# Attention feeding a gated feed-forward layer: 36 attention chunks in place of 40, load chains of their own, tile 2's gated sums kept on chip, and other figures in the ordering model

## The chip, the cores and the metric

The kernel runs on one core of a Trainium2 chip. The metric is the device time of one execution in microseconds (us), lower is better. Times are medians of several runs; the profile is that of one further execution.

## The reference

The attention of 8 batches, 8 heads, 576 queries of 64 elements looks at keys and values that are averaged over groups of 8, so 72 keys for each head. Its output, 4608 rows of 512, is the input of a feed-forward layer with two input matrices.

```python
k_p = k.reshape(B, H, Sp, 8, D).mean(axis=3)          # B, H, D = 8, 8, 64; S = 576; Sp = 72
v_p = v.reshape(B, H, Sp, 8, D).mean(axis=3)
scores = np.matmul(q, k_p.transpose(0, 1, 3, 2)) / np.sqrt(D)
attn = np.exp(scores - np.max(scores, axis=-1, keepdims=True))
attn = attn / (np.sum(attn, axis=-1, keepdims=True) + 1e-09)
x = np.matmul(attn, v_p).transpose(0, 2, 1, 3).reshape(4608, 512)
out = ((x @ w_a) * (x @ w_b)) @ w_out                 # 512 x 1536, 512 x 1536, 1536 x 512
```

## The kernel before

**Arithmetic.** Every matrix product is made of three matmuls in fp32r: each operand is split into a high part and a remainder (`hh` and `hl`, `xh` and `xl`, `qh` and `ql`), and high·high, high·low and low·high are summed in PSUM. ACT casts the high part (line 247, `copy`), and DVE or POOL subtracts it (line 225, `low_part` through `tt`).

**Feed-forward tiles.** The 4608 rows are nine tiles of 512 (t = 0 to 8); the 1536 inner columns are twelve chunks f of 128. "in t f" is 24 matmuls of 512 columns into the banks `psa` and `psb` (line 276, `pe`); `gate` multiplies the two banks into a gated sum; "out t f" is 12 matmuls into four `acc` banks. Tiles 0 and 1 are the opening, in which the weights arrive and are converted from 64-bit words (`convert_weights`), split (`split_weight`) and stored to DRAM as `jd` and `od`. Tile 2 is an ordinary tile that reads split weights back (`jab`, `jo_later` and `wo`). Tiles (3, 4), (5, 6) and (7, 8) are pairs, in which seven block products replace eight ("both p f", banks `bank_psa`, `bank_psb`, `bank_att`; `fold` adds them up on DVE, `fold_second` on POOL as `temp_p` and `temp_h`). The weights that these products need (`sums`, made by `sums_of_weights` of `wab`) are made once in tiles 1 and 2 and stored to `jd`; the sums of x (`sums_of_x`) are made ahead of each pair. The second tile of a pair, seven of tile 1's twelve gated sums and all of tile 2's are written to DRAM (`later<-gated`, `later<-temp_h`) and fetched again (`fetch_gated`, `back<-later`, then `hh` and `hl`).

**Attention.** `load_keys` and `load_values` pool a batch's k and v (`kraw`, `vraw`, two buffers `kv0` and `kv1`) and write the block-diagonal `kdiag` and `vdiag` (two of each, by batch parity). `chunk(i)` takes 128 or 64 queries: the load of `qraw`, split to `qh` and `ql`, two groups of 6 score matmuls (`psc`), maximum, exponential, sum and scaling on `s`, split to `pr` and `rem`, 10 transposes (`ptr`), and, once a block of up to 256 rows is whole, the value matmuls (`po`). A batch has 576 rows, so it is cut into four chunks of 128 and one of 64. Results go to `xh` and `xl` (tiles 0 and 1) or by `xo` to DRAM (`xd`).

**What sets the order.** The class `Schedule` (lines 71 to 180) issues all instructions of all engines from chains (Python generators) by a list scheduler: each operation has a modelled cost (line 53 on: `FIXED`, `EACH`, `BYTE`, `LAND`), and of those that can start within `SLACK` the one with the lowest rank goes first. Ranks come from `due`, the modelled time at which a step of the main chain falls. The engines then run their instructions in just that order; a wait of one holds all behind it. Operations that DVE and POOL both can do go to whichever the model says starts first. SP issues all DMAs through one queue. `tmps` is a pool of six 128x512 buffers, shared by `qraw`, `gated`, `back`, `xo`, `y` and others.

Of the kernel before, what the change touches and what calls it, by code (L numbers as in the profile page):

```python
# [17 lines left out]
POOL = 8  # L18
# [13 lines left out]
def chunks_of(b):  # L32
    sizes = [128, 128, 128, 128, 64] if b % 2 == 0 else [64, 128, 128, 128, 128]
    out, o = [], 0
    for n in sizes:
        out.append((o, n))
        o += n
    return out


# [5 lines left out]
NTMP = 6  # L46
LAG = 5

# [14 lines left out]
BYTE, LAND, AHEAD = 1 / 330e3, 1.4, 1.5  # L63


class Op:


    def __init__(self, engines, run, writes, reads, cost, rank=None, pair=False):
        self.engines, self.run, self.writes, self.reads = engines, run, writes, reads  # L70
        self.cost, self.rank, self.pair = cost, rank, pair
        self.end = None


class Schedule:
# [15 lines left out]
    def ready(self, op):  # L91
# [9 lines left out]
        return max(op.at, op.asked)  # L101
# [29 lines left out]
    def issue(self, engine, start, op):  # L131
# [5 lines left out]
        else:  # L137
# [10 lines left out]
            self.free[engine] = end  # L148
# [12 lines left out]

    def run(self):
# [26 lines left out]
def attn_moe_kernel(ctx: ExitStack, tc: tile.TileContext, q, k, v, vr, wa, wb, wo, out):  # L189
# [64 lines left out]
    def dma(out, in_, rank=None):  # L254
# [46 lines left out]
    def raw(name, f):  # L301
        if name == "o":
            return wo_first[:, f * 512:(f + 1) * 512] if f < 8 else wo_rest[:, (f - 8) * 512:(f - 7) * 512]
        at = (f % 4) * 1024 + (512 if name == "b" else 0)
        return wab[f // 4][:, at:at + 512]
# [6 lines left out]
    area = {name: work[:, x * 1024:(x + 1) * 1024] for x, name in enumerate(("a", "b", "o"))}  # L312

    flat = [(b, o, n) for b in range(B) for o, n in chunks_of(b)]
    tile_of = [(b * S + o) // NT for b, o, n in flat]
    early = sum(t == 0 for t in tile_of)
    blocks, start = [], 0

    def cut(chunks, limit):
        best = None  # L320
        for x in range(1, len(chunks) + 1):
            total = sum(flat[c][2] for c in chunks[:x])
            if total > limit:
                break
            cost, rest = cut(chunks[x:], limit) if x < len(chunks) else (0, [])
            cost += max(total, 2 * P)
            if best is None or cost < best[0]:
                best = cost, [chunks[:x]] + rest
        return best

    while start < len(flat):
        stop = start
        while stop < len(flat) and flat[stop][0] == flat[start][0] and tile_of[stop] == tile_of[start]:
            stop += 1
        blocks += cut(list(range(start, stop)), BLOCK)[1]
        start = stop
    block_of = [x for x, block in enumerate(blocks) for _ in block]
# [9 lines left out]
    streamed = {("o", t * NF + f) for t in [*range(2, STD), *(t1 for _, t1 in PAIRS)] for f in range(NF)}  # L347
# [35 lines left out]
    for t in range(2, STD):  # L383
        order += [("in", t, f) for f in range(NF)] + [("out", t, f) for f in range(NF)]
# [15 lines left out]
    stored |= {t * NF + f for t in [*range(2, STD), *(t1 for _, t1 in PAIRS)] for f in range(NF)}  # L400
    uses, upcoming = [], {name: [] for name in "aboh"}
    for kind, t, f in order:
# [16 lines left out]
    def chunk_due(i):  # L419
        b, o, n = flat[i]  # L420
# [5 lines left out]
        share = (b * S + o + n - group[0] * NT) / (NT * len(group))  # L426
# [4 lines left out]
    def queries(i):  # L431
        b, o, n = flat[i]
        return q[b, :, NK * o:NK * (o + n)].rearrange("p (g s) -> p g s", g=NK)

    def load_early():
        yield dma(early_q[:, 0, :, :flat[0][2]], queries(0))
# [4 lines left out]
        yield dma(early_q[:, 1, :, :flat[1][2]], queries(1))  # L441
# [5 lines left out]
        for i in range(2, early):  # L447
            yield dma(early_q[:, i, :, :flat[i][2]], queries(i))
            mark("early_q", i)

    def convert_weights(name):
        words = area[name].rearrange("p (c w) -> p c w", w=2)
        hi, lo = words[:, :, 1], words[:, :, 0]
        yield W(("early_q", early - 1))
        for f in range(NF):
            lead = due["in", 0, f] - (4.0 if name == "o" else 14.0) + (0.5 if name == "b" else 0.0)
            yield dma(area[name], w_dram[name][:, f, :].bitcast(I32), lead - 4.0)
# [6 lines left out]
            tag = yield from take(tmps)  # L464
            low = tmp(tag, f"wlow_{name}{f}", I32)
            one = act(w, hi.bitcast(F32), lambda: nc.scalar.activation(w, hi.bitcast(F32), AF.Abs, scale=SHRINK), lead)
            yield one
            yield act(low, lo, lambda: nc.scalar.activation(low, lo.bitcast(U32), AF.Copy, scale=2.0**-29), lead)
# [13 lines left out]
    holder, turn_of = {}, {"a": 0, "b": 0}  # L482
    spare, held = {}, {"o": 0, "h": 0}

    def buffer_of(name, x):
# [5 lines left out]
        return jab[n][:, "ab".index(name)]  # L491
# [19 lines left out]
    def split_weight(name, x):  # L511
# [10 lines left out]
        hi, lo = to[:, 0], to[:, 1]  # L522
# [735 lines left out]
```

## Time and profile before

| | |
|---|---|
| median of 3 runs | 1108.34 us (1105.13 to 1108.48) |
| the profiled execution | 1113.18 us |
| its span from first to last instruction | 1111.4 us |
| mean granted TensorE clock | 0.968 |
| TensorE matmuls (records) | 4936 |
| DMA | 262.55 MB, mean 236 GB/s |

The span falls into six stages, told by the first matmul of a kind on PE: the opening until `psa_0_0` (52.8 us), until tile 1 joins with `psa_1_5` (142.7 us), tiles 0 and 1 until `psa_2_0` (343.0 us), tile 2 until the first `bank_` (491.6 us), pair 0's products until the first `acc` of tile 4 (696.2 us), and the rest. Each row of a table by windows gives the stretch, its length, the busy time and number of instructions of PE, PEld (weight loads beside PE), DVE, ACT and POOL, the granted clock of TensorE, the mean busy share of the 16 DMA engines and the GB/s they moved. Rows of the chain of waits give start, length and what it was. A matmul's recorded time includes its passage through the array, so matmuls that follow one another overlap in the records, and PE's busy share says little; the spacing of starts is the price.

### The profile page before, as it was taken

The numbers are of one execution on the slowest core, as the hardware profiler recorded it, in microseconds if no ns is written. First come the engines' busy times: TensorE is split into PE (matmuls) and PEld (weight loads), VectorE is DVE, ScalarE is ACT, GpSimd is POOL, SyncE is SP. The second block draws the span as 40 slices with busy tenths as digits, with TensorE's granted clock in tenths as the row PEclk, the third lists the DMA queues.
The fourth block names the chain that finished last, engine by engine and source line by source line (L and its number), as shares of the span: only waits on it lengthen the run. The fifth ranks groups of instructions, "written<-read, shape, count | busy, mean of one in ns | idle before, by whom it ended". The sixth has DMA issues, their size and how long they took to land.

```text
span 1111.4 us, 14103 instructions
## 1 busy us (share of the span) xinstructions
PE 1032.5 (93%) x4936; PEld 842.1 (76%) x4936; DVE 651.3 (59%) x913; ACT 451.1 (41%) x897; POOL 386.6 (35%) x303
## 2 busy tenths in 40 slices
PE   2797799999989879899999999999999899999998
PEld 2676687788777768677788888688888688888876
DVE  7888788889667333867678865723333462333341
ACT  4665665566455333454455534521111331111121
POOL 5434343287363111813224413702211361111200
PEclk9797899999989989999999999999999999999999
DMA  6475378669998979687686756786667777666871
GB/s 204 134 257 182 109 238 280 201 211 322 309 316 306 311 257 323 225 286 235 210 254 219 242 201 206 254 272 207 210 221 266 265 244 251 217 215 201 284 236 68
DMA packets 130181, 262.55 MB, mean 236 GB/s; under 512 B 15776, under 2 KB 33696, under 8 KB 130112
## 3 DMA queue, kind: packets, MB, share of 16 engines
q1 hardware_dynamic: 130112, 261.66, 71.3%
q8 instruction: 39, 0.64, 0.2%
q14 instruction: 30, 0.25, 0.1%
HBM read 198.97 MB, written 62.65 MB: 235 GB/s over the span
## 4 chain that ended last, share of the span: by engine, by line
PE 62%; DMA 17%; DVE 11%; ACT 4%; issue 3%; SPq 1%; POOL 1%; ACTq 0%; POOLq 0%; DVEq 0%
PE acc L276 21%; PE bank_psb L276 12%; PE bank_att L276 8%; PE bank_psa L276 8%; PE psb L276 4%; DMA qraw<-in_q 3%; DMA vraw<-in_v 3%; PE psc L276 3%; PE po L276 3%; PE psa L276 3%; DMA vraw<-in_vr 2%; DMA kraw<-in_k 2%; DMA back<-later 2%; PE ptr L273 2%; SPq L258 1%
## 5 line engine op out<-in xcount | busy, mean ns | idle before, releaser
L276 PE MATMUL bank_psb<-x,j 128*128 128x512 f32 x648 | 167.3, 393 | 1.2 <-DVE temp L225 1.1
L276 PEld LDWEIGHTS bank_psb<-x,j 128*128 128x128 f32 x648 | 120.1, 188 | 27.1 <-DVE temp L225 1.7
L276 PE MATMUL bank_att<-x,j 128*128 128x512 f32 x432 | 111.2, 393 | 0.2 <-ACT temp L247 0.2
L276 PE MATMUL bank_psa<-x,j 128*128 128x512 f32 x432 | 111.3, 393 | 0.0
L276 PE MATMUL psb<-xh,jab 128*128 128x512 f32 x288 | 101.6, 409 | 6.4 <-ACT jab L247 3.3
L225 POOL TENSOR_TENSOR temp_p<-temp_p,temp 128x512 f32<-128x512 f32 x36 | 47.0, 1305 | 156.7 <-ACT temp_p L247 150.2
L276 PE MATMUL psa<-xh,jab 128*128 128x512 f32 x288 | 100.0, 404 | 1.2 <-POOL jab L225 1.2
L225 POOL TENSOR_TENSOR temp_h<-temp_h,temp 128x512 f32<-128x512 f32 x36 | 47.0, 1307 | 143.2 <-ACT temp_h L247 123.9
L276 PE MATMUL acc<-jo_later,hh 128*128 128x512 f32 x288 | 93.3, 405 | 0.1
L276 PEld LDWEIGHTS bank_att<-x,j 128*128 128x128 f32 x432 | 80.1, 188 | 17.5 <-ACT temp L247 0.7
L225 DVE TENSOR_TENSOR temp<-bank_psb,temp 128x512 f32<-128x512 f32 x72 | 49.7, 690 | 74.6 <-PE bank_psb L276 74.2
L276 PEld LDWEIGHTS bank_psa<-x,j 128*128 128x128 f32 x432 | 80.0, 188 | 17.0 <-ACT temp L247 0.3
L276 PE MATMUL acc<-wo,hh 128*128 128x512 f32 x240 | 80.5, 418 | 5.4 <-ACT hh L247 5.2
L225 DVE TENSOR_TENSOR temp<-bank_psa,temp 128x512 f32<-128x512 f32 x54 | 37.3, 691 | 73.3 <-PE bank_psa L276 72.5
L225 DVE TENSOR_TENSOR temp<-bank_att,temp 128x512 f32<-128x512 f32 x54 | 37.3, 691 | 72.0 <-PE bank_att L276 69.2
L276 PE MATMUL psc<-kdiag,qh 128*128 128x144 f32 (+1 forms) x320 | 62.3, 291 | 16.9 <-ACT kdiag L699 8.1
L225 POOL TENSOR_TENSOR ql<-qraw,qh 128x512 fp32r<-128x512 f32 (+1 forms) x35 | 43.2, 1237 | 98.6 <-ACT qh L247 95.3
L247 ACT CAST p<-ptr 128x512 fp32r<-128x512 f32 (+3 forms) x114 | 53.9, 476 | 46.8 <-PE ptr L273 45.8
L276 PEld LDWEIGHTS psc<-kdiag,qh 128*128 128x128 f32 (+1 forms) x320 | 53.9, 201 | 23.7 <-issue 7.9
L276 PEld LDWEIGHTS psb<-xh,jab 128*128 128x128 f32 x288 | 56.4, 196 | 19.8 <-ACT jab L247 3.8
L273 PEld LDWEIGHTS ptr<-ident,pr 128*128 128x128 f32 (+1 forms) x320 | 35.8, 146 | 45.2 <-ACT pr L247 28.6
L225 POOL TENSOR_TENSOR pr<-s,pr 128x512 fp32r<-128x512 f32 (+1 forms) x31 | 43.3, 1397 | 76.4 <-ACT pr L247 65.0
(143 smaller groups left out, 2219.8 us busy)
## 6 DMA issues: line engine op xcount, KB each, us to landing
j<-jd SPq DMA_DIRECT2D x108, 512.0 KB, 5.5
wo<-od SPq DMA_DIRECT2D x48, 512.0 KB, 5.9
jo_later<-od SPq DMA_DIRECT2D x36, 512.0 KB, 3.6
jab<-jd SPq DMA_DIRECT2D x34, 512.0 KB, 6.1
back<-later SPq DMA_DIRECT2D x55, 256.0 KB, 5.0
jd<-jab SPq DMA_DIRECT2D x24, 512.0 KB, 3.9
jd<-sums SPq DMA_DIRECT2D x24, 512.0 KB, 6.0
out<-y SPq DMA_DIRECT2D x36, 256.0 KB, 5.2
```

The source lines that it names most:

```text
L225: run = lambda e: vec[e].tensor_tensor(out=out, in0=in0, in1=in1, op=op)
L247: return act(out, in_, lambda: nc.scalar.copy(out, in_), rank)
L258: return Op((SD,), lambda e: nc.sync.dma_start(out, in_), [out], [in_], {SD: n * BYTE}, rank)
L273: nc.tensor.transpose(to, lhs, rhs)
L276: nc.tensor.matmul(to, lhs, rhs, start=start, stop=stop, skip_group_check=bool(skip))
```

## The change

It does these things:

- **Chunks.** 36 chunks of 128 rows over the 4608 flat rows, in 18 blocks of 256. Four chunks straddle two batches: they compute the scores twice (once for each batch's `kdiag`) and evict only the rows of each. Six blocks straddle, with value matmuls by row spans. The layout of q on the host follows.
- **Load chains.** k and v of batches 1 on are loaded by a chain `load_raw` ahead of their use, through the same two buffers; the words of the next weight are loaded by `load_words` as soon as the area has been read; `qraw` gets one buffer of its own (`qs`), and `NTMP` falls from 6 to 5. `fetch_gated` loads `back` before it claims its place for `hh` and `hl`, at most three ahead and leaving two `tmps`; its rank is ten us earlier.
- **Weights.** a and b of a chunk f are converted, split and loaded together ("ab", 1024 columns in an instruction). `od` is stored from tile 0's split and no longer from tile 1's.
- **Tile 2.** "in 2 f" and "out 2 f−1" alternate, so that the gated sums stay on chip; its `wo` comes through `jo_later` (`load_weight`) instead of a big buffer.
- **The ordering model.** A DMA costs `EVERY` more and lands later (`LAND` 1.4 to 1.8); attention operations on PE after tile 0 are ranked in only `MARGIN` (1.5 us) after their inputs; POOL leaves an operation to DVE if DVE, with what is queued for it, could start within `HELP` (1.5 us); the due times of tile 1's chunks, of the sums of weights and of the sums of x (12 us ahead of the pair instead of 25) are others.

Counted in the program's order, PE has 4898 matmuls and transposes in place of 4938 (360 `ptr` for 400; `psc`, `po` and the feed-forward are equal in number), DVE 980 instructions for 915, ACT 840 for 899, POOL 169 for 308, SP 637 DMAs for 668. `later<-gated` falls from 19 stores to 7, `back<-later` from 55 loads to 43.

```diff
-NTMP = 6
+NCH = B * S // P
+NTMP = 5
+JOIN, STEP = 40, 8
...
-BYTE, LAND, AHEAD = 1 / 330e3, 1.4, 1.5
+BYTE, EVERY, LAND, AHEAD = 1 / 330e3, 0.1, 1.8, 1.5
+MARGIN, HELP, AHEAD_F = 1.5, 1.5, 2
...
-        return max(op.at, op.asked)
+        return max(op.at + op.margin, op.asked)
...
+                    if e == SG and SV in entry[2].engines and self.free[SV] + self.backlog(start, entry) < start + HELP:
+                        continue
...
     for t in range(2, STD):
-        order += [("in", t, f) for f in range(NF)] + [("out", t, f) for f in range(NF)]
+        for f in range(NF):
+            order += [("in", t, f)] + ([("out", t, f - 1)] if f else [])
+        order.append(("out", t, NF - 1))
...
-    stored |= {t * NF + f for t in [*range(2, STD), *(t1 for _, t1 in PAIRS)] for f in range(NF)}
+    stored |= {t1 * NF + f for _, t1 in PAIRS for f in range(NF)}
...
         if t < 2:
-            return tile_due[t] - 40.0 + 0.01 * i
+            return (-20.0 + 0.01 * i) if t == 0 else JOIN + STEP * (i - early)
...
+    def load_raw():
+        yield W(("early_k", NK - 1))
+        for b in range(1, B):
+            for kind in "kv":
+                for x in range(NK if kind == "k" else NK + NG):
+                    at = yield from take(kv)
...
-            tag = yield from take(tmps)
+            tag = yield from take(qs)
             qraw = tmp(tag, f"qraw_{i}").rearrange("p (g s) -> p g s", g=NK)
...
         for g0 in range(0, NK, 2):
+            for b, lo, hi in flat[i]:
+                kd = kdiag[b % 2]
...
     def fetch_gated(x):
         yield W(("stored", x))
-        to = yield from place_for(x)
-        tag = yield from take(tmps)
+        yield lambda: x in upcoming["h"][:3]
+        tag = yield from take(tmps, 2)
         h = tmp(tag, f"back_{x}")
         yield dma(h, later.pop(x))
+        to = yield from place_for(x)
...
-        sch.spawn(sums_of_weights(), due["in", 2, 0] - 20.0 if STD > 2 else due["in", 1, 0])
+        sch.spawn(sums_of_weights(), due["in", 1, NF - 1])
...
-            sch.spawn(sums_of_x(p), due["both", p, 0] - 25.0)
+            sch.spawn(sums_of_x(p), due["both", p, 0] - 12.0)
```

Three places where the order differs. First SP's queue in the middle of tile 2. A row is a source line, the DMA and the tile it writes and reads; `wo2` is tile 2's big buffer before, `j0` pair 0's first weights, `x0` the x of pair 0. Before:

```order
L258 DMA later_30_3795<-gated_30_3790 128x512
L258 DMA back_24_3364<-later_24_3350 128x512
L258 DMA wo2_1_3792<-od4_106 128x1024
L258 DMA jab2_3008<-jd11_101 128x2x512
L258 DMA back_25_3448<-later_25_3430 128x512
L258 DMA wo2_1_3792<-od5_107 128x1024
L258 DMA later_31_3858<-gated_31_3856 128x512
```

After, at about the same step of tile 2:

```order
L261 DMA x0_2355<-xd4_116 128x1024
L261 DMA jo_later_3092<-od6_108 128x1024
L261 DMA j0_0_3804<-jd0_90 128x2x512
L261 DMA vraw_5_0_3746<-in_v 128x512
L261 DMA vraw_5_1_3864<-in_v 128x512
L261 DMA qraw_23_3744<-in_q 128x512
L261 DMA jab1_88<-jd10_100 128x2x512 x2
```

The stores and fetches of gated sums are gone; the loads for pair 0 (`x0`, `j0`) now stand amid tile 2's own loads, the latter ahead of `jab` for f = 10.

Second, the engine that makes the sums of weights, at its first chunks f in tile 1. Before, on POOL, among attention's `pr`, `s` and `ql`:

```order
L225 TENSOR_TENSOR sums_2104<-wab0_73 128x512
L225 TENSOR_TENSOR pr_11_2090<-s_11_1366,pr_11_2090 128x512
L225 TENSOR_TENSOR sums_2104<-wab0_73,sums_2104 128x256 x2
L225 TENSOR_TENSOR sums_2104<-sums_2104 128x1024
L225 TENSOR_TENSOR s_12_1826<-s_12_1826,z_12_1828 128x576
```

After, on DVE, among gating (`h`, `gated`), softmax and the splits of gated sums (`hl`):

```order
L228 TENSOR_TENSOR s_11_1659<-s_11_1659,z_11_1661 128x576
L228 TENSOR_TENSOR sums_2003<-sums_2003 128x1024
L228 TENSOR_TENSOR h_10_2019<-psb_0_10_2020,h_10_2019 128x512
L228 TENSOR_TENSOR sums_2003<-wab0_73 128x512
L228 TENSOR_TENSOR hl_10_2080<-h_10_2019,hh_10_2079 128x512
L228 TENSOR_TENSOR sums_2003<-wab0_73,sums_2003 128x256 x2
L235 SCALAR_TENSOR_TENSOR kdiag1_78<-kp_3_1475,kdiag1_78 64x2x72
L228 TENSOR_TENSOR gated_22_2111<-psb_1_10_2092,h_22_2094 128x512
```

All the sums of weights, the scaling of `s` and nearly all the low parts of `pr` have moved from POOL to DVE.

Third, PE where tile 2 ends and pair 0 begins. Before, the twelve "out 2" steps follow the last "in 2", and the row ahead of the first `bank_` is the last of them:

```order
L276 MATMUL acc_2_0_4097<-wo2_2_3898,hh_35_4464 128x512 x2
L276 MATMUL acc_2_0_4097<-wo2_2_3898,hl_35_4465 128x512
L276 MATMUL acc_2_1_4130<-wo2_2_3898,hh_35_4464 128x512 x2
L276 MATMUL acc_2_1_4130<-wo2_2_3898,hl_35_4465 128x512
L276 MATMUL acc_2_2_4143<-wo2_2_3898,hh_35_4464 128x512 x2
L276 MATMUL acc_2_2_4143<-wo2_2_3898,hl_35_4465 128x512
L276 MATMUL acc_2_3_4153<-wo2_2_3898,hh_35_4464 128x512 x2
L276 MATMUL acc_2_3_4153<-wo2_2_3898,hl_35_4465 128x512
L276 MATMUL bank_psa_4557<-x0_0_4099,j0_0_4235 128x512 x6
L276 MATMUL bank_psb_4558<-x0_4_4103,j0_0_4235 128x512 x6
```

After, between the last "in 2" and the first `bank_` stand 24 `acc` and 26 attention matmuls, and attention goes on among the products:

```order
L278 MATMUL ptr_26_0_4607<-ident_71,pr_26_4507 128x128 x4
L281 MATMUL acc_2_0_3288<-jo_later_3092,hh_35_4548 128x512 x2
L281 MATMUL acc_2_0_3288<-jo_later_3092,hl_35_4549 128x512
L281 MATMUL acc_2_1_3299<-jo_later_3092,hh_35_4548 128x512 x2
L281 MATMUL acc_2_1_3299<-jo_later_3092,hl_35_4549 128x512
L281 MATMUL acc_2_2_3314<-jo_later_3092,hh_35_4548 128x512 x2
L281 MATMUL acc_2_2_3314<-jo_later_3092,hl_35_4549 128x512
L281 MATMUL acc_2_3_3327<-jo_later_3092,hh_35_4548 128x512 x2
L281 MATMUL acc_2_3_3327<-jo_later_3092,hl_35_4549 128x512
L281 MATMUL bank_psa_4655<-x0_0_4525,j0_0_3804 128x512 x6
L278 MATMUL ptr_26_1_4665<-ident_71,pr_26_4507 128x128 x4
L281 MATMUL bank_psb_4656<-x0_4_4529,j0_0_3804 128x512 x6
```

What moved is the block of "out 2" matmuls: 120 of its 144 now stand ahead of the last "in 2" step.

More of the change, by code (lines that the diff above doesn't have):

```diff
@@ L29 @@
 SCALE = 1.0 / float(D) ** 0.5
[L32 to L38, printed above, removed]
 KM = D
@@ L160, in issue, with backlog @@
             op.run(engine)
+    def backlog(self, start, entry):
+        return sum(
+            x[2].cost[SV] for x in self.pending
+            if x is not entry and x[2].engines == (SV,) and x[:2] < entry[:2] and self.ready(x[2]) <= start + HELP
+        )
     def run(self):
@@ L311, in attn_moe_kernel, with rows_of @@
     work = place(sb, [P, 3 * 1024], I32, "work", "words")
-    area = {name: work[:, x * 1024:(x + 1) * 1024] for x, name in enumerate(("a", "b", "o"))}
-    flat = [(b, o, n) for b in range(B) for o, n in chunks_of(b)]
-    tile_of = [(b * S + o) // NT for b, o, n in flat]
+    area = {"ab": work[:, :2048], "o": work[:, 2048:]}
+    tile_of = [i * P // NT for i in range(NCH)]
     early = sum(t == 0 for t in tile_of)
[L317 to L337, printed above, removed]
+    def rows_of(lo, hi):
+        return [(b, max(lo, b * S) - lo, min(hi, b * S + S) - lo) for b in range(B) if b * S < hi and lo < b * S + S]
+    flat = [rows_of(i * P, i * P + P) for i in range(NCH)]
+    block_of = [i * P // BLOCK for i in range(NCH)]
     vrems, parts, xtiles, turned, later = {}, {}, {}, {}, {}
@@ L463, in convert_weights @@
             wi = w.bitcast(I32)
-            tag = yield from take(tmps)
[L465 to L468, printed above, removed]
+            lows = []
+            yield act(w, hi.bitcast(F32), lambda: nc.scalar.activation(w, hi.bitcast(F32), AF.Abs, scale=SHRINK), lead)
+            for n in range(len(name)):
+                tag = yield from take(tmps)
+                low, src = tmp(tag, f"wlow_{name[n]}{f}", I32), lo[:, n * 512:(n + 1) * 512]
+                lows.append((tag, low))
+                yield act(
+                    low, src,
+                    lambda low=low, src=src: nc.scalar.activation(low, src.bitcast(U32), AF.Copy, scale=2.0**-29), lead
+                )
             step = ts(wi, wi, 0x0FFFFFFF, 3, ALU.bitwise_and, ALU.logical_shift_left)
@@ L629, in sums_of_x @@
         mark("temps", p)
-        rank = due["both", p, 0] - 25.0
+        rank = due["both", p, 0] - 12.0
         def parted(c, src, mine):
@@ L720, in load_values @@
             else:
-                at = yield from take(kv)
-                vraw = place(sb, [P, S], F32, at, f"vraw_{b}_{x}")[:, :D * POOL]
-                if x < NK:
-                    yield dma(vraw, v[b, :, x, :])
-                else:
-                    yield dma(vraw[:NR], vr[b, :, x - NK, :])
+                yield lambda: ("v", b, x) in raws
+                vraw = raws["v", b, x]
             vv = vraw[:rows].rearrange("p (d j) -> p d j", j=POOL)
@@ L1149, in main @@
                 if t == 1:
-                    yield W(*(("value", block_of[i]) for i in range(len(flat)) if tile_of[i] == 1))
+                    yield W(*(("value", block_of[i]) for i in range(NCH) if tile_of[i] == 1))
                 elif t > 1:
```

323 lines of the change are left out of this document (174 added, 149 removed).

## The prediction

> **What bounds the kernel now.** I read the page first, then a table by windows at the six stage bounds, then the chain of waits in each stage. The page:
>
> ```profile
> span 1111.4 us, 14103 instructions
> PE 1032.5 (93%) x4936; PEld 842.1 (76%) x4936; DVE 651.3 (59%) x913; ACT 451.1 (41%) x897; POOL 386.6 (35%) x303
> ```
>
> TensorE leads, but its 93% counts overlapping records. So I price matmuls by their spacing. From the chain, two unbroken runs of one kind (start, length, what):
>
> ```profile
> 223.11 2.72 PE psb L276 x12
> 540.81 1.74 PE po L276 x16
> ```
>
> That is 0.227 us for a feed-forward matmul and 0.109 for a value matmul. From the timeline of PE, with nothing idle between the rows:
>
> ```profile
> 330.32 0.34 PE L276 MATMUL psc<-kdiag,qh 128*128 128x144 f32 x2
> ...
> 330.95 0.49 PE L273 MATMUL ptr<-ident,pr 128*128 128x128 f32 x4
> 331.28 0.71 PE L276 MATMUL acc<-jo_open,hh 128*128 128x512 f32 x2
> ```
>
> Six score matmuls start within 330.32 to 330.95, so 0.105 each, and four transposes within 0.33, so 0.08 each. The stages (stretch, length, busy of PE, PEld, DVE, ACT, POOL, clock, DMA share, GB/s), and as the last row the stretch in which DVE is fullest:
>
> ```profile
> 0.00:52.80 52.80, 25.82 (x133) 24.03 (x133) 40.07 (x60) 31.67 (x69) 26.77 (x34) 0.89 0.52 164
> 52.80:142.70 89.90, 74.30 (x352) 59.81 (x351) 74.05 (x113) 57.11 (x119) 35.43 (x28) 0.86 0.57 185
> 142.70:343.00 200.30, 192.41 (x967) 157.51 (x966) 160.53 (x215) 116.21 (x227) 105.77 (x78) 0.98 0.81 271
> 343.00:491.60 148.60, 134.47 (x664) 108.44 (x663) 80.53 (x112) 61.17 (x126) 41.67 (x32) 0.94 0.84 285
> 491.60:696.20 204.60, 200.32 (x1100) 165.44 (x1099) 143.61 (x223) 95.78 (x217) 71.54 (x58) 1.00 0.72 228
> 696.20:1111.40 415.20, 405.21 (x1730) 326.82 (x1728) 152.55 (x194) 89.21 (x141) 105.46 (x76) 0.99 0.68 227
> 59.50:315.20 255.70, 237.29 (x1176) 192.65 (x1175) 209.77 (x302) 154.92 (x314) 123.37 (x93) 0.95 0.72 241
> ```
>
> I counted the matmuls of each kind between the stage bounds in the program's order and multiplied by the four prices. Length less this work is what a stage loses:
>
> | stage | length | work | lost | work after |
> |---|---|---|---|---|
> | opening | 52.8 | 13.0 | 39.8 | 12.4 |
> | tile 0 alone | 89.9 | 59.1 | 30.8 | 58.9 |
> | tiles 0, 1 | 200.3 | 181.5 | 18.8 | 179.0 |
> | tile 2 | 148.6 | 120.7 | 27.9 | 134.3 |
> | pair 0 | 204.6 | 191.2 | 13.4 | 177.7 |
> | rest | 415.2 | 392.3 | 22.9 | 392.3 |
>
> For instance tile 2 has 432 x 0.227 for feed-forward, the rest attention. The sum is 957.8 of 1111.4: 154 us are lost, and only those are to be had, since the work changes by 40 transposes fewer, 40 x 0.08 = 3.2 us. What moves is attention worth 13.5 us, out of pair 0 into tile 2, where PE had room.
>
> **The change, stage by stage.**
>
> *Tile 2 (27.9 lost).* The chain of waits there:
>
> ```profile
> 416.63 5.29 DMA later<-gated
> 423.71 5.94 DMA qraw<-in_q
> 430.37 1.28 POOL ql L225
> 431.69 0.67 PE psc L276 x4
> ```
>
> A gated sum is stored; until its buffer comes free the next chunk's `qraw` cannot be loaded, and score matmuls stand in PE's queue behind it. PE is then idle long enough to cost clock as well:
>
> ```profile
> 405.45 0.70 PE L276 MATMUL psc<-kdiag,qh 128*128 128x144 f32 x2 [4.96 <-ACT qh L247]
> 400.00:420.00 20.00, 14.39 (x64) 12.14 (x63) 7.86 (x15) 5.09 (x10) 1.27 (x1) 0.74 0.77 266
> ```
>
> The change takes out the twelve stores and twelve fetches and gives `qraw` its own buffer. The new wait: that one buffer is loaded, split and only then loaded again, 5.94, ACT's cast until `ql` starts (429.65 to 430.37, 0.72) and 1.28, about 8 us a chunk; tile 2 has 150/12 = 12.5 chunks, 100 us of 148.6, so it is not the limit. Half of what is lost goes: 27.9 to 14. Behind the waiting `qraw` on SP's queue stand `jab` and `jo_later`, which now carry the alternating steps; if the queue remains the limit, all 27.9 stay. On the other side, "out 2" was a block of 144 x 0.227 = 32.7 us, behind which the sums of x for pair 0 were made; now 24 feed-forward and 26 attention matmuls (8.1 us) stand between the last "in 2" and the first product. About 24 operations of 0.69 us on DVE (16.6 us) must be done there, shared by two engines; less 8.1 and with the first product needing only a part of them, I take 4 us (0 to 8). So 134.3 + 18 = 152.3.
>
> *Tile 0 alone (30.8 lost).* The pieces of the chain that bring k and v:
>
> ```profile
> 71.36 5.01 DMA kraw<-in_k
> ...
> 79.55 5.24 DMA kraw<-in_k
> ...
> 96.55 2.80 DMA vraw<-in_v
> ...
> 104.21 3.62 DMA vraw<-in_vr
> ```
>
> Loads stand in the chain for 16.7 us because the chain that pools also issues them. `load_raw` takes them out, but through the same two buffers, so of ten loads for a batch only two can wait in place. I take two thirds, 11 us: 30.8 to 20. Chunks of tile 1 also come earlier on PE (amid `psa_0_1` in place of `psa_0_3`); what they fill was idle. The merged "ab" conversion makes `psa` wait for both halves: the low part of 1024 columns on DVE is twice 0.69, about the 1414 ns that POOL took for 512 (below), so nothing. If k and v still come last, 31; if all goes, 11.
>
> *Opening (39.8 lost).*
>
> ```profile
> 40.70 3.95 DMA qraw<-in_q
> ...
> 44.67 0.62 ACT qh L247
> ```
>
> The 3.95 of `qraw` waits for a buffer and stands on ACT ahead of `pr` of the last early chunk; it goes. But DVE's work up to the first `psb` eviction, priced at 0.69 per 512 columns and 0.75 for a reduction of 576, grows from 36.7 to 46.1 us, as work comes from POOL. DVE is busy 40.07 of 52.8 already. I let the two cancel nearly: 39 (35 to 48). So 51.4.
>
> *Tiles 0 and 1 (18.8 lost).* POOL's work goes to DVE here: sums of weights, `jab`, `s`, `pr`. By-form groups (operation, count, busy, mean ns, idle before):
>
> ```profile
> L225 POOL TENSOR_TENSOR jab<-wab,jab 128x512 fp32r<-128x512 f32 x20 | 28.3, 1414 | 61.5 <-ACT jab L247 61.5
> L225 DVE TENSOR_TENSOR hl<-temp,hh 128x512 fp32r<-128x512 f32 x36 | 24.9, 692 | 20.4 <-ACT hh L247 20.1
> L225 DVE TENSOR_TENSOR hl<-back,hh 128x512 fp32r<-128x512 f32 x37 | 40.2, 1089 | 27.1 <-ACT hh L247 26.9
> L240 DVE TENSOR_REDUCE z<-s 128x8 f32<-128x576 f32 x32 | 23.9, 747 | 7.0 <-ACT s L807 6.9
> ```
>
> An operation that costs POOL 1414 ns costs DVE 692. Between the first `psb` eviction and the eviction of `psb_1_4` (59.5 to 315.2 us) DVE's priced work rises from 178 to 206 us. Measured it was 209.77, 1.18 times its price. The same subtraction takes 692 ns on one source and 1089 on another, which I read as POOL reading SBUF beside the latter. With POOL's instructions nearly halved (308 to 169) I expect some 1.1: 227 us of about 245, 93%. DVE is then very full, but the added work is the sums, of low rank, not due before pair 0. What PE gains by the loads it loses in DVE's queue: lost 18. So 197.
>
> The Trainium skill, page "SBUF — State Buffer", section "Who interferes with whom", says that a DVE instruction with two SBUF inputs contends with a GpSimd instruction that reads SBUF, and that the second of them fully blocks. 692 against 1089 ns agrees; by that rule alone DVE would be at its 206 us, this stage would lose some 4 us less, and the sum would be about 4 lower.
>
> *Pair 0 and the rest.* Pair 0 has 13.5 us less attention among its products, so fewer chances to be late: 13.4 to 11, 177.7 + 11 = 188.7 (188 to 191). In the rest the fetch of a gated sum stands in the chain near the end of a pair:
>
> ```profile
> 880.55 5.41 DMA back<-later
> ...
> 1074.45 4.22 DMA back<-later
> ```
>
> `back` is now loaded before its place is free and up to three ahead; of these 9.6 us I take 6, since the last products' sums cannot be fetched before they exist: 22.9 to 17, so 409.3 (404 to 415).
>
> *Sum:* 51.4 + 78.9 + 197 + 152.3 + 188.7 + 409.3 = 1077.6 of span. The profiled execution's time lies 1.8 above its span (1113.18), so 1079.4; the median lies at 1108.34/1113.18 = 0.9957 of the profiled one, so 1074.7, **1075 us**. The unknown ends (−4 to +9, ±10, −4 to +5, −18 to +14 with the sums of x, −1 to +2, −5 to +6), added as squares, give about ±22.
>
> **The rivals.** *A. The DMA queue stays the limit in tile 2.* Its row has the highest DMA share of all, 0.84 at 285 GB/s. The 24 transfers of 0.26 MB that go (6.3 MB) are 15% of 148.6 us x 285 GB/s = 42 MB, but `x0` and `j0` move in. Then 27.9 + 4 stay lost there, +14: **1089**. Against it: the chain there is a wait for a buffer, not a full queue.
>
> *B. The clock comes back too.* PE's busy time by one less the clock is 2.8 in the opening, 10.4 in tile 0 alone, 8.1 in tile 2. If no stretch idles for long any more (clock 0.98 there), 1.5 and 2.7 remain of the latter two: 14 us more: **1061**. The clock is low where PE idles in pieces of five us:
>
> ```profile
> 98.68 0.69 PE L273 MATMUL ptr<-ident,pr 64*128 64x64 f32 x4 [5.31 <-ACT pr L247]
> 100.00:120.00 20.00, 15.49 (x66) 12.70 (x66) 14.12 (x24) 10.76 (x26) 7.55 (x7) 0.67 0.42 140
> ```
>
> The Trainium skill, "TensorE: Matmul & The Clock Gate", section "What's actually happening", has this as a gate: half clock after an idle window of about 3.4 us, full after a busy one. These rows agree; which of the idle pieces stay above that length, no row of before can tell.
>
> *C. DVE becomes the bound (slower).* If the ratio of 1.18 stays, DVE needs 206 x 1.18 = 243 us between 59.5 and 315.2. At the 82% it is busy now (209.77 of 255.7) that is 296 us, +41, while the other stages give −1.4 in the opening, +3.7 in tile 2, −15.9 and −5.9 in the last two, −19.5 in all: +21, **1130**. It turns slower where DVE cannot get above 243/(255.7 + 19.5) = 88% there. For it: DVE's queue is in order, and PE's gating (`h`, `gated`) now stands behind sums. Against it: POOL's own work causes the excess.
>
> *D. The change does little:* the model's new figures only shuffle waits, **1108**. The order speaks against it, since stores, fetches and POOL's work do go.
>
> **How the numbers follow.** Forecast 0.56, A 0.18, B 0.12, C 0.11, D 0.03. The forecast's own ±22 is 1053 to 1097. The range takes in B with some 13 of its own spread below, and A with some 15 above: 1048 to 1104; C, D and the tails stay out, about 0.2. A measurement of this kernel tells 0.3% (3.3 us) from no change. Faster by more: forecast, A and B, 0.86; within: D, 0.03; slower: C, 0.11.
>
> **What would show it.** Right: in the windows at the same marks, tile 2 loses some 18 us instead of 27.9 and no `qraw` of five us stands behind a store in its chain; k and v are gone from tile 0's chain; DVE above 88% from 59.5 on with PE's lost time not higher; the sums of x show as a wait of PE of some 4 us at the first `bank_`. A would show as DMA share still at 0.84 in tile 2 with `jab` or `qraw` last; B as a clock of 0.95 or more in every stage; C as `psb` waiting for `h` or `gated` on DVE between 60 and 315 us. The forecast is wrong if the stage of tiles 0 and 1 grows, or if what tile 2 gains is lost at the start of pair 0.

## The result and the profile after

The changed kernel takes 1058.91 us (median of 4 runs, 1054.74 to 1064.53) beside 1107.61 for the kernel before: a ratio of 0.9567, 95% interval 0.9511 to 0.9623. Timed again in more rounds (E12) the ratio was 0.9583 (0.9551 to 0.9614). The profiled execution took 1054.74, the lowest of its four. Its page, first lines and the summary of the chain of waits:

```profile
span 1052.6 us, 13699 instructions
...
PE 1006.1 (96%) x4896; PEld 834.4 (79%) x4896; DVE 640.0 (61%) x978; ACT 438.8 (42%) x838; POOL 212.7 (20%) x164
...
PE 85%; DVE 6%; ACT 3%; DMA 3%; issue 1%; SPq 0%; POOL 0%; ACTq 0%; DVEq 0%; POOLq 0%
```

The last of these lines had PE 62% and DMA 17% before: DMA has all but left the chain. The windows at the same six marks, and as the last row the stretch between the first `psb` eviction and that of `psb_1_4`:

```profile
0.00:50.40 50.40, 25.15 (x126) 23.59 (x126) 42.81 (x66) 31.73 (x67) 19.04 (x26) 0.90 0.57 195
50.40:128.50 78.10, 70.43 (x347) 58.28 (x347) 68.86 (x103) 53.77 (x103) 16.48 (x12) 0.87 0.74 246
128.50:313.20 184.70, 183.87 (x940) 153.17 (x941) 168.34 (x251) 113.47 (x208) 34.73 (x23) 1.00 0.84 287
313.20:452.40 139.20, 139.20 (x802) 119.05 (x801) 92.79 (x167) 75.50 (x165) 13.16 (x10) 1.00 0.86 280
452.40:643.00 190.60, 186.07 (x960) 154.90 (x959) 115.01 (x185) 76.41 (x159) 45.39 (x34) 0.98 0.67 216
643.00:1052.60 409.60, 401.34 (x1729) 325.38 (x1727) 152.17 (x209) 87.95 (x141) 83.91 (x60) 0.99 0.69 229
58.90:292.90 234.00, 225.54 (x1136) 187.23 (x1135) 212.26 (x317) 148.12 (x273) 46.64 (x32) 0.96 0.82 280
```

Length less priced work gives what each stage loses, as in the prediction. All kernels of the study in the order told below (E12, the changed kernel profiled once more, shows how far a stage varies: up to 3 us in tile 0 alone and the rest, under 1 in the others). The spans gain 58.8 us where the medians gain 48.7, because the kernel before was profiled in an execution slower than the four that give its median (1113.18) and the changed one in its fastest:

| lost, us | opening | tile 0 alone | tiles 0, 1 | tile 2 | pair 0 | rest | median |
|---|---|---|---|---|---|---|---|
| before | 39.8 | 30.8 | 18.8 | 27.8 | 13.4 | 23.0 | 1107.61 |
| forecast | 39 | 20 | 18 | 18 | 11 | 17 | 1075 |
| changed | 38.1 | 19.1 | 5.8 | 4.8 | 12.9 | 17.4 | 1058.91 |
| E1 POOL back | 37.2 | 33.0 | 11.5 | 3.8 | 13.7 | 20.5 | 1074.03 |
| E2 loads back | 37.6 | 22.4 | 18.8 | 3.9 | 18.3 | 17.0 | 1074.85 |
| E3 tile 2 back | 38.8 | 18.7 | 7.0 | 4.2 | 6.8 | 17.9 | 1049.94 |
| E4 margin 0 | 38.4 | 21.9 | 6.0 | 6.7 | 17.8 | 20.8 | 1064.83 |
| E5 tile 2 and loads back | 39.0 | 26.3 | 15.2 | 6.8 | 5.7 | 14.2 | 1065.21 |
| E6 no prefetch of k, v | 39.1 | 29.5 | 5.6 | 4.5 | 13.7 | 18.3 | 1064.63 |
| E7 sums of x early | 38.1 | 19.4 | 5.7 | 4.5 | 13.0 | 20.0 | 1056.65 |
| E8 before, with HELP | 36.1 | 27.9 | 20.7 | 34.3 | 11.9 | 23.0 | 1115.95 |
| E9 E5 and old figures | 39.0 | 27.7 | 8.7 | 8.6 | 12.8 | 18.4 | 1070.83 |
| E10 E5 and old buffer rules | 38.8 | 23.7 | 21.1 | 20.6 | 9.8 | 21.0 | 1092.82 |
| E11 old buffer rules alone | 38.8 | 18.9 | 16.6 | 4.2 | 15.8 | 25.4 | 1074.28 |
| E12 changed again | 38.9 | 22.1 | 6.0 | 4.8 | 12.6 | 19.9 | 1060.45 |

Four stages came out within 2 us of the forecast. The two in the middle lost 12.2 and 13.2 us less, which is the whole miss of 25 us of span (16 us of the median). Tile 2's chain holds nothing but PE (its shares by line):

```profile
by line: PE acc L281 25.1%; PE psb L281 24.5%; PE psa L281 24.2%; PE psc L281 11.6%; PE po L281 9.4%; PE ptr L278 5.4%
```

### The profile page after: what moved, and what is told of

Its sections match the earlier page's. It is cut to its first block, busy times and chain, and to the rows that moved or that the text cites. A ratio compares the mean times of both kernels' runs of the same rounds, so it can differ in the third digit from the quotient of the medians.

```text
span 1052.6 us, 13699 instructions
## 1 busy us (share of the span) xinstructions
PE 1006.1 (96%) x4896; PEld 834.4 (79%) x4896; DVE 640.0 (61%) x978; ACT 438.8 (42%) x838; POOL 212.7 (20%) x164
## 4 chain that ended last, share of the span: by engine, by line
PE 85%; DVE 6%; ACT 3%; DMA 3%; issue 1%; SPq 0%; POOL 0%; ACTq 0%; DVEq 0%; POOLq 0%
PE acc L281 26%; PE bank_psb L281 14%; PE bank_psa L281 9%; PE bank_att L281 9%; PE psb L281 8%; PE psa L281 8%; PE po L281 4%; PE psc L281 4%; PE ptr L278 2%; DMA words<-in_wo 1%; DMA vraw<-in_v 1%; DVE s L228 1%; ACT x L250 1%; DMA words<-in_wb 1%; DVE temp L228 1%
## 5 line engine op out<-in xcount | busy, mean ns | idle before, releaser
L281 PE MATMUL acc<-jo_later,hh 128*128 128x512 f32 x384 | 124.2, 405 | 0.2
L281 PE MATMUL psa<-xh,jab 128*128 128x512 f32 x288 | 102.5, 409 | 5.7 <-ACT jab L250 2.8
L228 POOL TENSOR_TENSOR ql<-qraw,qh 128x512 fp32r<-128x512 f32 x28 | 39.4, 1407 | 219.7 <-ACT qh L250 214.9
L281 PEld LDWEIGHTS acc<-jo_later,hh 128*128 128x128 f32 x384 | 68.5, 189 | 13.0 <-ACT hh L250 1.5
L281 PE MATMUL acc<-jo_later,hl 128*128 128x512 f32 x192 | 76.3, 398 | 0.0
L250 ACT CAST p<-ptr 128x512 fp32r<-128x512 f32 (+1 forms) x102 | 52.3, 514 | 48.1 <-PE ptr L278 47.9
L250 ACT CAST hh<-temp 128x512 fp32r<-128x512 f32 x36 | 22.4, 621 | 119.1 <-DVE temp L228 119.1
L281 PEld LDWEIGHTS psa<-xh,jab 128*128 128x128 f32 x288 | 55.7, 194 | 19.9 <-ACT jab L250 3.5
L281 PE MATMUL psc<-kdiag,qh 128*128 128x144 f32 x320 | 62.7, 292 | 7.6 <-ACT kdiag L737 7.0
L281 PEld LDWEIGHTS psc<-kdiag,qh 128*128 128x128 f32 x320 | 56.5, 210 | 11.2 <-issue 7.0
```

The lines of the kernel that those rows point to most:

```text
L228: run = lambda e: vec[e].tensor_tensor(out=out, in0=in0, in1=in1, op=op)
L250: return act(out, in_, lambda: nc.scalar.copy(out, in_), rank)
L281: nc.tensor.matmul(to, lhs, rhs, start=start, stop=stop, skip_group_check=bool(skip))
```

## The experiments

**E1. POOL takes its work back.**

```diff
-                    if e == SG and SV in entry[2].engines and self.free[SV] + self.backlog(start, entry) < start + HELP:
-                        continue
```

> The changed kernel without the rule by which POOL leaves work to DVE (HELP); 285 instructions on POOL in place of 169, the sums of weights and most low parts of pr among them. Theory 1 (POOL's own reading slows DVE, and this is why tiles 0 and 1 lose 5.8 us where 18 were forecast): between the first psb eviction and that of psb_1_4 DVE is no more than 1.03 times its priced work in the changed kernel, and goes back to 1.12 or more here; the subtraction for a fetched gated sum (hl from back) goes from 737 ns to 950 or more; tiles 0 and 1 lose 12 to 20 us; 1067 to 1078 us in all. Rival (the gain in tiles 0 and 1 comes from the load chains or from the model's margin, and which of the two engines does the work is of no account): tiles 0 and 1 lose 4 to 8 us as in the changed kernel, 1055 to 1063 us.

It took 1074.03 us, ratio 0.9716 (0.9682 to 0.9750). Its fetched gated sums by form, then its window between the same evictions, then the changed kernel's fetched sums by form. After each group of fetched sums stands one of the same size that reads one of its two inputs from PSUM:

```profile
L226 DVE TENSOR_TENSOR hl<-back,hh 128x512 fp32r<-128x512 f32 x29 | 30.8, 1062 | 29.4 <-ACT hh L248 29.4
L226 DVE TENSOR_TENSOR h<-psb,h 128x512 f32<-128x512 f32 x29 | 19.9, 688 | 28.9 <-PE psb L279 28.8
```

```profile
56.20:308.60 252.40, 233.94 (x1169) 194.82 (x1168) 211.32 (x262) 152.48 (x283) 135.11 (x89) 0.94 0.79 266
```

```profile
L228 DVE TENSOR_TENSOR hl<-back,hh 128x512 fp32r<-128x512 f32 x29 | 21.4, 737 | 22.8 <-ACT hh L250 19.1 <-PE acc L281 3.7
L228 DVE TENSOR_TENSOR h<-psb,h 128x512 f32<-128x512 f32 x29 | 19.9, 687 | 6.9 <-PE psb L281 6.7
```

Theory 1 holds for contention. DVE's priced work in this stretch is 167.1 us in E1 and 206.1 in the changed kernel, yet it is busy 211.3 and 212.3: 1.26 and 1.03 times the price. DVE does 39 us more priced work in the same busy time when POOL is busy 47 us beside it and not 135. Only the operation with both inputs in SBUF slows, from 737 to 1062 ns; the one that reads PSUM takes 687 and 688. But the rule is worth some 15 us (14 against E12), and most of that lies in tile 0 alone: 13.9 us, or 10.9 against E12. Tiles 0 and 1 lost 11.5, just under the 12 expected. In tile 0 alone PE waits longest for POOL itself, whose low part of `jab` takes about twice DVE's time:

```profile
PE psa L279 <- POOL jab L226: 5.3, 4, 2.2
```

The Trainium skill, page "SBUF — State Buffer", section "Who interferes with whom", has a DVE instruction with two SBUF inputs contend with a GpSimd instruction that reads SBUF; 1062 against 737 ns for one subtraction agrees.

**E2. The loads as before** (no `load_raw`; `qraw` from the six common buffers):

```diff
-NTMP = 5
+NTMP = 6
...
-                    yield lambda: ("k", b, g) in raws
-                    kraw = raws["k", b, g]
+                    at = yield from take(kv)
+                    kraw = place(sb, [P, S], F32, at, f"kraw_{b}_{g}")
+                    yield dma(kraw, k[b, :, g, :])
...
-            tag = yield from take(qs)
+            tag = yield from take(tmps)
...
-        sch.spawn(load_raw(), 0.0)
```

> The changed kernel with the loads as before: k and v issued by the chain that pools them, qraw out of the common buffers, of which there are six again. Theory 2 (the load chains are what frees PE's queue of late score matmuls in tile 2, 27.9 lost to 4.8, and they give the 11 us of tile 0 alone): tile 2 loses 15 to 28 us and its clock falls to 0.97 or less, tile 0 alone loses 27 to 33, 1075 to 1092 us. Rival (in tile 2 it is the gated sums that stay on chip, and in tile 0 alone the earlier words of the weights): tile 2 loses 4 to 9 us, tile 0 alone 18 to 23, 1057 to 1066 us.

1074.85 us, ratio 0.9725 (0.9696 to 0.9755): the time at the edge of what theory 2 gives, in the wrong places. Tile 2 lost 3.9 us and tile 0 alone 22.4, both as the rival has them; tiles 0 and 1 lost 18.8, as much as before. There PE's longest wait is for `qh`, behind a late `qraw`, and the clock falls with it (waits, chain, the stage's window, then two windows behind the wait):

```profile
PE psc L281 <- ACT qh L250: 5.1, 1, 5.1
```

```profile
294.37 6.64 DMA qraw<-in_q
```

```profile
131.60:333.30 201.70, 195.91 (x978) 165.19 (x978) 169.87 (x258) 117.49 (x219) 39.63 (x26) 0.95 0.81 270
```

```profile
306.00:310.00 4.00, 4.00 (x21) 4.00 (x20) 3.94 (x5) 2.15 (x5) 2.22 (x2) 0.50 0.41 96
314.00:318.00 4.00, 4.00 (x19) 3.90 (x18) 2.26 (x5) 0.57 (x1) 0.00 (x0) 0.50 0.40 107
```

Of the 18.8 us, 15.5 are lost between 290 and 333 us, around that one wait: some 5 us of waiting, and behind it some 20 us at half clock (0.69 from 298, 0.50 from 302 to 318, 0.75 to 322), which cost some 10 more.

**E3. Tile 2 as before** (twelve "in", then twelve "out"; gated sums stored; `wo` in big buffers):

```diff
-        for f in range(NF):
-            order += [("in", t, f)] + ([("out", t, f - 1)] if f else [])
-        order.append(("out", t, NF - 1))
+        order += [("in", t, f) for f in range(NF)] + [("out", t, f) for f in range(NF)]
...
-    stored |= {t1 * NF + f for _, t1 in PAIRS for f in range(NF)}
+    stored |= {t * NF + f for t in [*range(2, STD), *(t1 for _, t1 in PAIRS)] for f in range(NF)}
...
-        todo = [("x", 0)]
+        todo = [("wo", 2, c) for c in range(3)] + [("x", 0)]
```

> The changed kernel with tile 2 as before: twelve in steps, then twelve out steps, its gated sums stored to DRAM and fetched, its wo in big buffers. Theory 2 (load chains) expects tile 2 and pair 0 to lose 18 to 24 us together as in the changed kernel (17.7), so 1057 to 1066 us, less what the block of out steps saves at the first product (the sums of x, up to 4 us). Rival (the gated sums on chip make the gain of tile 2): tile 2 loses 15 to 25 us by itself, DMA share at 0.84 or more, 1070 to 1083 us.

1049.94 us, ratio 0.9498 (0.9463 to 0.9533): faster than the changed kernel, whose interval in E12 lies clear of it. Tile 2 loses 4.2 us even at a DMA share of 0.87 (0.84 before), and pair 0 loses 6.8 in place of 12.9. The changed kernel's chain at the start of pair 0, then its waits there and its window, then E3's waits in its pair 0 (whole list) and its window of tile 2:

```profile
453.21 1.44 ACT x L250 x2
...
455.00 1.99 ACT x L250 x2
...
457.83 0.75 PE ptr L278 x4
```

```profile
PE ptr L278 <- ACT s L250: 3.9, 1, 3.9
PE bank_psb L281 <- DVE temp L228: 0.5, 1, 0.5
```

```profile
452.40:462.40 10.00, 6.08 (x24) 4.91 (x23) 7.39 (x11) 6.86 (x11) 4.41 (x3) 0.72 0.56 185
```

```profile
PE bank_att L281 <- DVE temp L228: 0.6, 1, 0.6
```

```profile
314.80:437.00 122.20, 121.50 (x637) 102.03 (x636) 71.66 (x108) 55.32 (x112) 20.13 (x13) 1.00 0.87 289
```

So this part of the change costs some 9 us (1058.91 or 1060.45 less 1049.94), and some 6 of them are at the start of pair 0: over its first 20 us of priced work the changed kernel loses 7.8 us, E3 1.4. There ACT splits the sums of x (`x` in the chain) ahead of attention's `p` and `s`, a transpose waits for it, and the clock falls. The block of "out 2" matmuls was cover for the sums of x. The remaining 3 us are no more than a stage varies. Tile 2 loses no more with its gated sums stored and fetched, so the traffic that the change saves was not on the chain.

**E4. MARGIN at 0.**

```diff
-MARGIN, HELP, AHEAD_F = 1.5, 1.5, 2
+MARGIN, HELP, AHEAD_F = 0.0, 1.5, 2
```

> The changed kernel with MARGIN at 0, so that attention's operations on PE stand where the model has their inputs just ready. Theory 3 (the margin keeps PE from standing behind attention whose inputs come later than modelled): the waits of PE for qh, ql, pr and p come back in tiles 0 and 1 and in tile 2, which together lose 20 to 30 us where the changed kernel loses 10.6; 1068 to 1080 us. Rival (inputs come when the model says, since the load chains and DVE's steadier times took the lateness away): 9 to 14 us lost there, 1055 to 1063 us.

1064.83 us, ratio 0.9636 (0.9601 to 0.9670). The two stages together lose 12.7 us: the rival's 9 to 14, though the whole lies just above its range. The 4 to 6 us come from pair 0 (17.8), where PE waits for the sums of x themselves, and smaller pieces:

```profile
PE bank_psb L281 <- DVE x L228: 5.0, 2, 3.6
```

**E5. E2 and E3 together.**

> The changed kernel with tile 2 as before (gated sums stored and fetched) and the loads as before (no load_raw, qraw out of the six common buffers) at once. Either alone left tile 2 losing 4 us. Theory (each of the two removes the wait of qraw for a buffer that a gated sum holds, so the one hides what the other is worth): with both back tile 2 loses 14 to 28 us as before, its clock falls under 1.00, 1083 to 1100 us. Rival (what emptied tile 2 of waits is POOL's exit from the chain of chunks and the model's figures, which are still in): tile 2 loses 4 to 8 us; the time is the sum of the two single runs, 1074.85 less 7, 1063 to 1073 us.

1065.21 us, ratio 0.9634 (0.9590 to 0.9678). The theory fails: tile 2 loses 6.8. Something else in the change suffices. In tiles 0 and 1 E2's late `qraw` is back (15.2 lost, 11.9 of them between 295 us and the end of the stage).

**E6. Only the prefetch of k and v undone** (E2 with `qraw` left in its own buffer).

> The changed kernel with k and v issued by the chain that pools them, but qraw in its own buffer. With both load chains back the kernel took 1074.85 us. If the prefetch of k and v is what is worth that (some 17 us, most of it in tiles 0 and 1): 1069 to 1078 us, tiles 0 and 1 lose 15 us or more. If it is the buffer of qraw: 1055 to 1063 us, tiles 0 and 1 lose 5 to 9.

1064.63 us, ratio 0.9631 (0.9590 to 0.9672), between the two expectations. Tiles 0 and 1 lose 5.6, so their 13 us in E2, that is the one wait, hang on the buffer of `qraw`. Tile 0 alone loses 29.5, so the prefetch is worth 10 us there, or 7 against E12, near the 11 that the prediction took for it, and 4 to 6 in the whole. But E2 lacks it too and lost 22.4 there, no more than E12; how the two interact stays open.

**E7. Sums of x ranked 25 us ahead, x loaded 40 us ahead.**

```diff
-                        yield dma(to[:, r, n:n + HALF], xd[t][:, n:n + HALF], due["both", at, 0] - 28.0)
+                        yield dma(to[:, r, n:n + HALF], xd[t][:, n:n + HALF], due["both", at, 0] - 40.0)
...
-        rank = due["both", p, 0] - 12.0
+        rank = due["both", p, 0] - 25.0
...
-            sch.spawn(sums_of_x(p), due["both", p, 0] - 12.0)
+            sch.spawn(sums_of_x(p), due["both", p, 0] - 25.0)
```

> The changed kernel with the sums of x ranked 25 us ahead of each pair, and x loaded 40 us ahead, as before. Pair 0 loses 12.9 us in the changed kernel, 3.9 in one wait of PE for ACT at its start; with the block of out steps back ahead of it, it lost 6.8. Theory (the sums of x have lost their cover): made earlier, they are ready, pair 0 loses 6 to 10 us, 1050 to 1056 us. Rival (pair 0 loses it to attention among its products, not to the sums of x): pair 0 loses 11 to 14 us, and tile 2 loses what the earlier sums push back: 1057 to 1064 us.

1056.65 us, ratio 0.9548 (0.9497 to 0.9598), no different from the changed kernel; pair 0 loses 13.0, 7.5 of them in its first 20 us of work. The wait of 3.9 us for ACT is gone, but the products now wait for `x` from DVE (1.4 us) and POOL (0.5), and the clock is 0.67 over the first 10 us. A rank does not help: in the code `sums_of_x` waits until the last "in 2" is issued, since its buffers are that step's operands. Of what was tried, only work put behind that step (E3) covers them.

**E8. The kernel before, with HELP alone** (the rule and `backlog` added, nothing else).

> The kernel before with one thing alone of the change: POOL leaves an operation to DVE if DVE could start it within 1.5 us. Undone in the changed kernel it cost 17 us, 14 of them in tile 0 alone. If what it is worth does not hang on the rest (POOL's slow operations and its contention with DVE), the kernel gains 12 to 20 us: 1085 to 1094 us, tile 0 alone loses 18 to 24 us in place of 30.8. If it pays only once k and v come early: 1100 to 1108 us, tile 0 alone loses 27 or more.

1115.95 us, ratio 1.0091 (1.0054 to 1.0129): slower by 0.9%. Both expectations miss: tile 0 alone gains 3 us and tile 2 loses 34.3. The two profiled executions are equally long (1111.6 and 1111.4 us), so the table shows where E8 gains and loses, but not its 0.9%. In tile 2 one wait stands out, around which 16.5 of the 34.3 us are lost; the longest in the kernel before is 5.0 us there (the window of tile 2, PE's longest wait in it, then DVE's timeline before that, idle time in brackets):

```profile
344.20:496.60 152.40, 130.24 (x639) 104.60 (x637) 80.17 (x127) 57.42 (x121) 21.69 (x14) 0.92 0.79 260
```

```profile
PE psb L285 <- DVE gated L234: 14.4, 1, 14.4
```

```profile
372.53 0.69 DVE L249 TENSOR_REDUCE vp<-vraw 128x64 f32<-128x512 f32 x1 [3.46 <-DMA vraw<-in_v]
380.28 0.69 DVE L249 TENSOR_REDUCE vp<-vraw 128x64 f32<-128x512 f32 x1 [7.07 <-DMA vraw<-in_v]
381.63 0.69 DVE L234 TENSOR_TENSOR hl<-back,hh 128x512 fp32r<-128x512 f32 x1 [0.67 <-ACT hh L256]
382.36 0.69 DVE L234 TENSOR_TENSOR gated<-psb,h 128x512 f32<-128x512 f32 x1
```

DVE stands twice at the head of its queue for a load of v, and the gating that would free `psb` is queued behind.

**E9. E5 with the old figures of the ordering model too** (MARGIN, EVERY, LAND, the due times; HELP stays).

> The kernel with tile 2 and the loads as before (1065.21 us, tile 2 loses 6.8) and now also the ordering model's figures: MARGIN 0, no EVERY, LAND 1.4, the due times of tile 1's chunks, of the sums of weights and of the sums of x as before. HELP, the 36 chunks, the merged conversion and the rules for the common buffers stay. Theory (the figures are what empties tile 2: a later landing and a margin put PE's work behind what really comes late): tile 2 loses 18 us or more, 1085 to 1110 us. Rival (the rules for the common buffers, or the 36 chunks, do it): tile 2 loses 5 to 10 us, 1064 to 1076 us.

1070.83 us, ratio 0.9666 (0.9612 to 0.9720); tile 2 loses 8.6. The figures do not empty tile 2, and are worth some 6 us in all here, not clear of the intervals. Tiles 0 and 1 lose only 8.7: in this order no late `qraw` stands in PE's queue there, though `qraw` comes out of the common buffers as in E2 and E5.

**E10. E5 with the old rules for the common buffers.**

```diff
-        tag = yield from take(tmps, 1)
+        tag = yield from take(tmps)
...
     def fetch_gated(x):
         yield W(("stored", x))
-        yield lambda: x in upcoming["h"][:3]
-        tag = yield from take(tmps, 2)
+        to = yield from place_for(x)
+        tag = yield from take(tmps)
         h = tmp(tag, f"back_{x}")
         yield dma(h, later.pop(x))
-        to = yield from place_for(x)
...
-                    sch.spawn(fetch_gated(x), due[kind, t, f] - 20.0)
+                    sch.spawn(fetch_gated(x), due[kind, t, f] - 10.0)
```

> The kernel with tile 2 and the loads as before, the new figures kept, and the rules for the common buffers as before: no chain leaves a buffer free for others, and a fetched gated sum claims its place before its load, ten us later. Theory (these rules keep a buffer free for qraw, so that it does not wait for a gated sum's store): tile 2 loses 15 us or more and qraw stands behind a store in its chain again, 1078 to 1095 us. Rival (the model's figures do it): tile 2 loses 5 to 9 us, 1062 to 1070 us.

1092.82 us, ratio 0.9872 (0.9804 to 0.9940). Tile 2 loses 20.6 and tiles 0 and 1 lose 21.1 (before: 27.8 and 18.8). The size is the theory's, the mechanism only half: no `qraw` behind a store, but loads at the head of DVE's queue again (wait, then the chain that leads to it):

```profile
PE psb L281 <- DVE gated L228: 6.8, 1, 6.8
```

```profile
352.99 7.62 DMA vraw<-in_v
...
361.34 4.16 DMA vraw<-in_v
...
367.28 6.55 DMA back<-later
...
374.50 0.70 DVE hl L228
...
375.30 0.70 DVE gated L228
```

What this version still gains on the kernel before, 1.3%, is due to the rest of the change: HELP, the figures, the 36 chunks, the merged conversion and `load_words` among it. The last three were undone in no run.

**E11. The old buffer rules alone, in the changed kernel** (E10's edit, without E5's).

> The changed kernel with the rules for the common buffers alone as before: no chain leaves a buffer free, a fetched gated sum claims its place before its load and ten us later. With tile 2 and the loads as before too, these rules cost 28 us, 14 of them in tile 2. Theory (tile 2 has three covers for the same shortage of buffers: the gated sums on chip, the buffer of qraw, the rules, and the first two do without the third): tile 2 loses 4 to 8 us; the rest loses 18 to 23 by later fetches; 1056 to 1066 us. Rival (the rules are needed by themselves): tile 2 loses 12 us or more, 1070 to 1085 us.

1074.28 us, ratio 0.9702 (0.9658 to 0.9747). Tile 2 loses 4.2 as the theory has it, but the whole does not: the rules are worth some 15 us elsewhere (against E12: 10.6 in tiles 0 and 1, 5.5 in the rest), and in the rest PE waits for the split of a late fetch:

```profile
PE acc L281 <- DVE hl L228: 4.0, 1, 4.0
PE acc L281 <- ACT hh L250: 3.4, 4, 1.7
```

**E12. The changed kernel again.**

> The changed kernel unaltered, timed in more rounds, since its first four runs spread over 9.8 us, and the kernel with tile 2 stored took 1049.94 us. If storing tile 2's gated sums and its block of out steps is in truth faster than keeping them on chip: a ratio to the kernel before of 0.953 to 0.960, clear of 0.9498. If the two are the same: 0.947 to 0.952.

1060.45 us, ratio 0.9583 (0.9551 to 0.9614), within the first of the two expectations: E3 is the fastest version of the study.

## Why the prediction was right, point by point

**Direction and range: right, low in the range.** 1058.91 lies between 1048 and 1104, at the time of rival B (1061) rather than of the forecast (1075). Four terms of the sum hold; two are 12 and 13 us too high, both in the same direction.

**Opening, tile 0 alone, pair 0, rest: right in size** (38.1, 19.1, 12.9, 17.4 for 39, 20, 11, 17). For tile 0 alone the prefetch was credited with 11 us and is worth 7 to 10 in E6, though nothing in E2; but POOL's exit, which the prediction left at nothing there ("so nothing" for `jab`), is worth 11 to 14 in the same stage (E1). The two overlap, since the whole gain is 11.7. The loads of k are gone from this stage's chain as foretold, but one `vraw` of 4.42 us still stands in it. Pair 0's size is luck: its 12.9 us hold some 6 for the sums of x, which the prediction had put into tile 2, so attention among the products costs about 7 (E3: 6.8) where 11 were taken. In the rest the buffer rules with the earlier fetch of gated sums are worth 5.5 (E11 against E12), near the 6 that were taken. The opening's terms were not tested.

**Tiles 0 and 1: the step that failed** is "what PE gains by the loads it loses in DVE's queue: lost 18". DVE was indeed filled to 91% (212.26 of 234.00), but at 1.03 of its price where 1.1 was taken, and a full DVE did not hold PE up: PE lost 5.8 us. So what the loads give was not lost there. In the changed kernel it takes `qraw`'s own buffer (18.8 lost without, E2 against E6) and the rules for the other common buffers (16.6 without, E11), both of which the prediction had given to other stages; E9, without the first, loses only 8.7. But the wait that the kernel before had is neither of these. Half of its 18.8 us, 9.7, is lost behind 315 us, where PE stands for `vdiag` and `vrem` behind late loads of v (chain, then PE's longest wait in the stage):

```profile
299.47 4.86 DMA vraw<-in_vr
...
305.07 6.08 DMA vraw<-in_vr
```

```profile
PE po L276 <- DVE vrem L225: 2.6, 1, 2.6
```

No version made from the changed kernel has this wait in this stage at more than 0.3 us, not even E6 without the prefetch of v. Which part of the change removed it stays open.

**Tile 2: the size was wrong and the reason too narrow.** "Half of what is lost goes" was 23 of 27.8. The prediction named the stored gated sums and `qraw`'s buffer. Undoing both leaves 6.8 lost (E5); the old buffer rules on top bring 20.6 back (E10), and those rules alone do not (E11, 4.2). The changed stage has more than one cover for the same fault, loads that come late while other work is queued behind them. Of the rules' three parts (a buffer left free, the load ahead of the claim, ten us earlier) none was tried by itself.

**The sums of x: foreseen, but in the neighbouring stage and dearer.** The 4 us put into tile 2 show as the 3.9 us wait at pair 0's start, and E3 removes it. With the clock that falls behind the wait they cost some 6 (7.8 less 1.4).

**Rival A** is refuted: DMA share in tile 2 rose to 0.86, 0.87 in E3, with PE losing under 5 us. **Rival B** gives nearly the measured time by half of its mechanism: the clock went from 0.94 to 1.00 in tile 2 but only from 0.86 to 0.87 in tile 0 alone. By the prediction's product, PE's busy time by one less the clock, 8 us came back in tile 2 and 4 in tiles 0 and 1 (192.41 x 0.02), of the 36 that the two stages gained; the rest is waits. Rival B's 14 us also counted all of tile 2's clock, part of which the forecast's halving had taken already. The rule of the Trainium skill, "TensorE: Matmul & The Clock Gate", section "What's actually happening" (half clock after an idle window of about 3.4 us), agrees with E2's stretch, a wait of 5.1 us and then 0.50, beside the changed kernel's 1.00 in the same stage, where no listed wait is over 1 us. The full clock after a busy window of that length, which the same section of the Trainium skill states too, did not come so soon in E2: it stayed at 0.50 from 306 to 318 us with PE's records unbroken.

**Rival C** did not come true: DVE reached 91%, above the 88% under which it had the kernel slower, and needed 212 us where it took 243, since it held the ratio of 1.18 fixed. Between 60 and 313 us the longest listed wait of `psb` for DVE is 0.4 us. E8 is a neighbouring case and not C itself: the same move of work to DVE, in a kernel whose loads come late, is 0.9% slower, with DVE busy 53% of the stage in which PE stands for it.

## What to carry to other kernels

Price an engine's added work together with the contention it takes away, and look at what stands at the head of an in-order queue rather than at its busy share: DVE at 91% went with 5.8 us lost in tiles 0 and 1, and at 53% (80.17 of 152.40, E8's tile 2) it held TensorE up for 14 us. When a stage has several covers for one shortage, undoing each alone shows nothing; undo them together before saying which one works. Work that is moved out of a block may have been the cover of something behind that block. And price a wait of PE with the clock that falls behind it: E2's one wait of 5.1 us cost some 15.

## What the runs showed of the hardware

In the stretch between the two evictions DVE and POOL gave little more together than DVE alone: with POOL busy 135 us beside it DVE finished 167 us of priced work in 211 busy us, with POOL busy 47 us it finished 206 in 212. The 88 us more of POOL are, by 1414 against 692 ns for one operation, an estimated 43 us of DVE's work, and DVE lost 39.

Behind a wait of PE of 5.1 us the granted clock was 0.50 for 16 us and more (E2); behind one of 3.9 us the mean over 10 us was 0.72 (the changed kernel), and without such a wait 1.00 (E3, its first 10 us of pair 0).

The DMA engines at a mean share of 0.87 and 289 GB/s (E3's tile 2) held nothing up, where a share of 0.79 and 260 GB/s (E8's) went with a stall of 14 us: in these two the share does not tell whether a given load is late.
